# The weight of every key in columns of its own, with another order of work in the first batch: hashed attention followed by a gated feed-forward layer on one core

## The chip, the core and the metric

One NeuronCore of a Trainium2 chip runs the whole program. The metric is the time of the device in microseconds (us). The engines named below are TensorE (PE, with its weight loads listed as PEld), VectorE (DVE), ScalarE (ACT), GpSimd (POOL) and SyncE (SP), whose queue issues most of the DMAs. Each engine works through its own list of instructions in order and waits for the others by semaphores.

## The reference

```python
# q, k, v: 4 batches x 8 heads x 768 tokens x 64; proj: 64 x 6
q_bits = (einsum('bhsd,dk->bhsk', q, proj) > 0)      # 6 sign bits for each token
k_bits = (einsum('bhsd,dk->bhsk', k, proj) > 0)
mask   = bucket(q_bits)[..., :, None] == bucket(k_bits)[..., None, :]
scores = where(mask, q @ k.T / 8, -1e9)
attn   = softmax(scores)          # exp(s - max) / (sum + 1e-9)
x      = (attn @ v) as 3072 tokens x 512
g, val = x @ w_gate, x @ w_val                        # 512 -> 1536 each
ffn    = (gelu(g) * val) @ w_out                      # 1536 -> 512
out    = x + sigmoid(x @ w_res) * ffn
```

A query attends only to the keys of its own bucket. Where a query's bucket holds no key, every score is -1e9, and the softmax gives every key the same weight. The kernel needs a device for this case, and it is the part that the change rebuilds.

## The kernel before

The heads are worked in 16 pairs: pair `p` is two heads of batch `p // 4`. A pair of heads fills 128 partitions, 64 for each head. For each pair the work is as follows.

- `load` brings q, k and v from HBM (384 KB each, on SP's queue). `cast` (POOL, 0.82 us) makes bf16 copies of q and k.
- `transpose_dma` turns the bf16 copies over by a transposing DMA on SP's queue (pairs 0 and 1 use `transpose_pe` on TensorE); the result is `aug`. `move_second` (POOL) copies the second head's half into a tile `second`.
- `blocks` (DVE) transposes the fp32 data in small blocks; `hash_half` (PE) multiplies it by `projw`, a block matrix made from `proj`, and DVE turns the signs into `hb`. `spread` (PE, then a DVE copy into `bits`) lays the bits out as seven rows for each head and side, and `mask_rows` carries these rows by four small DMAs (10.5 KB each) next to the 64 rows of `aug` and into `second`. Scores of the pair can only begin when they have landed.
- `scores` runs chunk by chunk: two to four matmuls into one of two PSUM tiles `sp`, then one exp on ACT into `e` (1.02 us for 1024 columns). The seven extra rows push the score of a pair of unequal buckets far down, so that its exp is nothing.
- `values_cast` and `values_sum` (POOL) make v in bf16 with a column of ones beside it (`va`), and the sum of v over the six key tiles (`vsum`). `values` multiplies `e` by `va` and adds up in the PSUM tile `av`: for each head six query tiles of 64 values and one row sum, 390 columns.
- Before the first chunk of a head, one matmul opens the accumulation: `eps_sb`, a 128x128 tile full of 2^-90, times `vsum`. It adds the tiny weight 2^-90 for every key to every query, and so gives the mean of v where no key matches. The same 65 columns are wanted for all six query tiles, so it streams 390 columns, six times the same.
- `finish` (DVE) takes the reciprocal of the row sums and multiplies, into `x_tok`. Then `x_transpose` turns `x_tok` over into `x_sb`: in the first batch and for the last pair of a batch on TensorE with a DVE copy, otherwise by a DMA on SP's queue.

When a batch's four pairs are done, `gate_val` runs the two wide products of the feed-forward layer (for each of the two weights 48 matmuls of 512 columns and 48 of 256) with Gelu on ACT and the product on DVE. `project` (for each of six token tiles 4 matmuls `rps` for the gate, Tanh on ACT, and 12 matmuls `fps`) is a generator: `mlp_matmuls` takes a few of its matmuls at a time into the slots of the next batch's attention.

The order on each engine is the program's order: it is written out by hand. A slot is one chunk of a pair: 12 in pair 0 (one head at a time, 768 columns), 9 in every other pair. `at(slot, f, ...)` hangs a task on a slot; the main loop at the end issues a slot's scores, its tasks, some `mlp_matmuls` by a budget (`fill`), then the values of the chunk one or two slots back (`flush`). `LEAD = 4` slots of the next batch come ahead of `gate_val`, and `HELD` is the number of `project`'s matmuls that are kept back to lie beside the `finish` of the last pair. `base(p)` is the first slot of pair `p`.

Names and lines that matter here: `scores` L403 with its matmul at L408 and exp at L412; `values` L376 with the opening matmul at L385 and the others at L390; `finish` L353 to L363 (reciprocal L360, product L361); `x_transpose` L365; `mask_rows` L312 with its DMA at L319; `load` L81, its DMA at L89; `move_second` L202 (copy L204); `transpose_dma` L198 (L199); `gate_val` L417 (matmul L427, Gelu L433, product L436); `project` L441 (L449, Tanh L452, L459, L464, and the residual add on POOL L466); the table of tasks L548 to L647; the budget L649 to L663; the main loop L665 to L694. The opening matmul is

```python
nc.tensor.matmul(o, eps_sb,
    vsum[:, hi, 0:D + 1].unsqueeze(1).to_broadcast([P, T, D + 1]),
    start=True, stop=False, skip_group_check=True)
```

## Time and profile before

| what | us |
|---|---|
| five runs | 360.55, 360.68, 361.10, 362.20, 362.96; median 361.1 |
| the profiled execution: time of the device | 363.73 |
| its span in the profile | 362.0 |
| 0 to 9.1: loads, first pair's preparation, until the first exp | 9.1 |
| 9.1 to 58.2: the first batch's attention | 49.1 |
| 58.2 to 90.4, 141.9 to 174.0, 225.8 to 257.9, 306.2 to 336.6: `gate_val` of the four batches | 32.2, 32.1, 32.1, 30.4 |
| 90.4 to 141.9, 174.0 to 225.8, 257.9 to 306.2: attention of batches 1 to 3 with `project` of the batch before | 51.5, 51.8, 48.3 |
| 336.6 to 362.0: the last `project` | 25.4 |

The span is the stretch that the profile covers; the device's time is 1.73 us longer. A profile page gives busy times for each engine, the chain of waits that ended last, and groups of equal instructions with the mean of one in nanoseconds (ns). A busy time of TensorE counts the ends of overlapping matmuls, so the distance between the starts of two matmuls says more than their durations.

### The profile page before, as it was taken

How to read it: one execution, taken by the hardware profiler on the slowest of the kernel's cores; microseconds unless marked ns; L12 is line 12 of the kernel's file. 1: busy time of each engine (PE TensorE's matmuls, PEld its weight loads, DVE VectorE, ACT ScalarE, POOL GpSimd, SP SyncE). 2: the span in 40 equal slices, each digit the busy share in tenths (PEclk: the TensorE clock that was granted, in tenths of full speed). 3: DMA queues.
4: the chain of work that ended last, by engine and by line, in shares of the span. 5: the costliest groups of instructions: out<-in, count | busy, mean ns of one | idle time of the engine just before them, and what ended most of it. 6: DMA issues, size and time to landing. Idle time of an engine off the chain costs nothing.

```text
span 362.0 us, 7500 instructions
## 1 busy us (share of the span) xinstructions
PE 344.2 (95%) x3040; PEld 202.9 (56%) x3089; DVE 145.6 (40%) x213; ACT 211.3 (58%) x239; POOL 138.1 (38%) x185
## 2 busy tenths in 40 slices
PE   7896989999999999999999999999999999999994
PEld 4554565665465566666455556665555655666442
DVE  7861644333344334434343434334442123333343
ACT  5885887234788787232877777332778885232210
POOL 5978853866447258300046547400025112000000
PEclk9998999999999999999999999999999999999999
DMA  7879849997904952830003964510002210000012
GB/s 219 260 148 218 238 150 351 328 314 197 256 32 122 217 173 87 215 117 0 2 3 83 199 214 132 120 40 3 0 2 61 83 51 31 29 2 0 31 60 86
DMA packets 52574, 44.06 MB, mean 122 GB/s; under 512 B 31640, under 2 KB 44348, under 8 KB 52540
## 3 DMA queue, kind: packets, MB, share of 16 engines
q1 hardware_dynamic: 52396, 43.56, 42.8%
q8 instruction: 24, 0.39, 0.4%
q14 instruction: 10, 0.08, 0.1%
q0 software_dynamic: 64, 0.02, 0.0%
q10 hardware_dynamic: 80, 0.00, 0.0%
HBM read 29.36 MB, written 6.29 MB: 99 GB/s over the span
## 4 chain that ended last, share of the span: by engine, by line
PE 83%; DMA 5%; ACT 4%; SPq 2%; POOL 2%; issue 2%; DVE 2%; DVEq 0%; ACTq 0%; POOLq 0%
PE sp L427 34%; PE fps L459 17%; PE sp L408 13%; PE av L390 8%; PE rps L449 5%; DMA ld<-in_q_dram 3%; ACT e L412 3%; PE hs L270 3%; SPq L89 2%; PE spr L283 2%; DMA aug<-bits 1%; PE av L385 1%; ACT th L452 1%; DVE o L464 1%; DVE x_tok L361 1%
## 5 line engine op out<-in xcount | busy, mean ns | idle before, releaser
L412 ACT ACTIVATE e<-sp 128x1024 bf16<-128x1024 f32 (+1 forms) x147 | 145.0, 1007 | 40.4 <-PE sp L408 32.8
L433 ACT ACTIVATE gt<-sp 128x768 bf16<-128x768 f32 x48 | 38.9, 810 | 83.2 <-PE sp L427 83.2
L436 DVE SCALAR_TENSOR_TENSOR hh<-gt,sp 128x768 bf16<-128x768 bf16 x48 | 45.8, 954 | 81.7 <-PE sp L427 81.7
L459 PE MATMUL fps<-wo,hh 128*128 128x512 bf16 x276 | 72.7, 378 | 0.7
L390 PEld LDWEIGHTS <-e 128*128 128x128 bf16 x1152 | 52.3, 98 | 32.6 <-issue 11.2
L427 PE MATMUL sp<-x_sb,wg 128*128 128x512 bf16 (+1 forms) x377 | 70.0, 325 | 0.5
L427 PE MATMUL sp<-x_sb,wv 128*128 128x512 bf16 (+1 forms) x375 | 69.8, 324 | 0.5
L466 POOL TENSOR_TENSOR o<-o,x_tok 128x512 f32<-128x512 f32 x18 | 20.8, 1154 | 122.1 <-issue 69.4
L408 PE MATMUL sp<-aug,aug 71*128 71x512 bf16 x192 | 55.1, 330 | 5.6 <-DMA aug<-bits 3.0
L390 PE MATMUL av<-va,e 128*128 128x65 bf16 x1152 | 59.0, 194 | 1.2 <-ACT e L412 0.5
L427 PEld LDWEIGHTS <-wg 128*128 128x128 bf16 x384 | 37.4, 98 | 24.9 <-issue 0.3
L427 PEld LDWEIGHTS <-wv 128*128 128x128 bf16 x384 | 37.3, 98 | 24.5
L408 PE MATMUL sp<-second,second 128*128 128x256 bf16 (+1 forms) x174 | 47.9, 323 | 0.2
L459 PEld LDWEIGHTS <-hh 128*128 128x128 bf16 x288 | 27.6, 97 | 27.7
L464 DVE SCALAR_TENSOR_TENSOR o<-th,fps 128x512 f32<-128x512 f32 x24 | 16.4, 685 | 56.2 <-PE fps L459 54.6
L204 POOL COPY second<-aug 64x768 bf16<-64x768 bf16 x30 | 24.3, 826 | 18.0 <-DMA aug<-nat 16.1
L233 DVE STREAM_TRANSPOSE t<-ld 128x768 f32<-128x768 f32 (+1 forms) x34 | 30.0, 910 | 1.2 <-DMA ld<-in_q_dram 1.1
L449 PE MATMUL rps<-wr,x_sb 128*128 128x512 bf16 x93 | 24.5, 379 | 0.2
L452 ACT ACTIVATE th<-rps 128x512 f32<-128x512 f32 x24 | 14.3, 595 | 16.3 <-PE rps L449 13.0
L408 PEld LDWEIGHTS <-aug 71*128 71x128 bf16 x192 | 16.1, 98 | 9.0 <-DMA aug<-bits 3.2
L408 PEld LDWEIGHTS <-second 128*128 128x128 bf16 x192 | 18.7, 98 | 4.3 <-issue 1.4
L290 DVE CAST bits<-spr 128x512 bf16<-128x512 f32 (+1 forms) x24 | 15.5, 653 | 11.5 <-PE spr L283 11.3
(59 smaller groups left out, 226.1 us busy)
## 6 DMA issues: line engine op xcount, KB each, us to landing
ldv<-in_v_dram SPq DMA_DIRECT2D x16, 384.0 KB
out_dram<-o SPq DMA_DIRECT2D x24, 256.0 KB
ld<-in_q_dram SPq DMA_DIRECT2D x15, 384.0 KB
ld<-in_k_dram SPq DMA_DIRECT2D x15, 384.0 KB
ws<-in_moe_w_gate_dram SPq DMA_DIRECT2D x6, 512.0 KB
ws<-in_moe_w_val_dram SPq DMA_DIRECT2D x6, 512.0 KB
ws<-in_moe_w_out_dram SPq DMA_DIRECT2D x6, 512.0 KB
ws<-in_moe_w_res_dram SPq DMA_DIRECT2D x2, 512.0 KB
```

What stands on the lines that cost most here:

```text
L204: eng.tensor_copy(second[x[0] % NM][x[1]][D:P], aug[x][D:P])
L233: nc.vector.transpose(t32[x][:, c0:c1].rearrange("p c h n -> p (c h n)"), raw[x][:, c0:c1].rearrange("p c d -> p (c d)"))
L390: nc.tensor.matmul(o[:, qt0 + i, :], e[:, off + i * P:off + (i + 1) * P], va[:, hi, jt, 0:D + 1], start=False, stop=(jt == T - 1), skip_gr ...
L408: nc.tensor.matmul(sp[:, off:off + nq * P], ks[0:n, jt, :], qs[0:n, qt0:qt0 + nq, :], start=True, stop=True)
L412: nc.scalar.activation(e[:, 0:n], sp[:, 0:n], AF.Exp, scale=float(ALPHA))
L427: nc.tensor.matmul(sp[:, c0:c1], w[:, kk, bass.ts(m, P)], xs[:, kk, c0:c1], start=(kk == 0), stop=(kk == KM - 1))
L433: nc.scalar.activation(gt, sp[:, 0:S], AF.Gelu)
L436: nc.vector.scalar_tensor_tensor(hh[:, m, :], gt, 0.5, ps[1][:, 0:S], op0=ALU.mult, op1=ALU.mult)
L449: nc.tensor.matmul(rps, x_sb[b][:, kk, t, :], wr[:, kk, :], start=(kk == 0), stop=(kk == KM - 1))
L459: nc.tensor.matmul(fps, hh[:, m, bass.ts(t, P)], wo[:, m, :], start=(m == 0), stop=(m == KF - 1))
L464: nc.vector.scalar_tensor_tensor(o, th, 1.0, fps, op0=ALU.add, op1=ALU.mult)
L466: last.tensor_add(o3, o3, x_tok[b][:, :, t, :])
```

## The change

Four things are changed together.

1. From the second batch on, the opening matmul of a head no longer streams 390 columns into the accumulators. It writes 65 columns of its own behind them in the same PSUM bank. At the end of the pair DVE copies these 65 columns of both heads to SBUF (`share`), adds them to all six query tiles (`total`, in SBUF), and takes the reciprocal. The product into `x_tok` goes to POOL for the first three pairs of a batch and stays on DVE for the last. The first batch keeps the old form (`whole(p)`).
2. `x_transpose` of those pairs comes later: in slot 6 of the next pair instead of 4, or slot 3 instead of 2 at a batch's end. In `gate_val` the last values of the lead slots are issued ahead of the fourth k-slice of the first product instead of behind it, and 15 matmuls instead of 12 are held back for the last batch.
3. The start: `projw` is made by one POOL product from a broadcast load of `proj` and a striped tile; the first head of pair 0 is transposed alone, ahead of the hash, and ACT copies both results; the second head's cast of q goes from ACT to POOL. There are 6 warming matmuls instead of 15.
4. The table of the first batch: pair 1's steps and pair 2's casts come one slot later, some loads earlier or later (the loads of v of pair 2 and of q and k of pair 4 in slot 7 instead of 9; those of pair 5 behind the mask rows of pair 2 instead of ahead of them), `move_second` of pair 3 four slots later, the values of pair 2 earlier and of pair 3 later. `values_sum` works in place and drops an unused branch.

```diff
+    o2_pool = ctx.enter_context(tc.tile_pool(name="sums", bufs=1))
-    proj_sb = const.tile([D, NBITS], FP32, name="proj_sb")
-    nc.scalar.dma_start(proj_sb, proj)
+    proj4 = const.tile([P, 2, NBITS], FP32, name="proj4")
+    for dh, eng in ((0, nc.scalar), (1, nc.gpsimd)):
+        eng.dma_start(proj4[:, dh], proj[32 * dh:32 * dh + 32].unsqueeze(0)
+                      .to_broadcast([4, 32, NBITS]))
...
+    def whole(p):
+        return p < HP
...
-        o = av.pop(p)[:, :, 0:T * (D + 1)].rearrange("p h (t d) -> p h t d", t=T)
+        acc = av.pop(p)
+        n = T * (D + 1)
+        o = acc[:, :, 0:n].rearrange("p h (t d) -> p h t d", t=T)
+        eng = nc.vector
+        if not whole(p):
+            share = sm_pool.tile([P, 2, D + 1], FP32, tag="share", name="share")
+            nc.vector.tensor_copy(share, acc[:, :, n:n + D + 1])
+            total = o2_pool.tile([P, 2, T, D + 1], FP32, tag="total", name="total")
+            nc.vector.tensor_add(total, o,
+                                 share.unsqueeze(2).to_broadcast([P, 2, T, D + 1]))
+            o = total
+            if hp < HP - 1:
+                eng = nc.gpsimd
         rec = sm_pool.tile([P, 2, T], FP32, tag="rec", name="rec")
         nc.vector.reciprocal(rec, o[:, :, :, D])
-        nc.vector.tensor_mul(x_tok[b][:, hp].rearrange("p t (h d) -> p h t d", h=2),
-                             o[:, :, :, 0:D],
-                             rec.unsqueeze(3).to_broadcast([P, 2, T, D]))
+        eng.tensor_mul(x_tok[b][:, hp].rearrange("p t (h d) -> p h t d", h=2),
+                       o[:, :, :, 0:D], rec.unsqueeze(3).to_broadcast([P, 2, T, D]))
...
-                nc.tensor.matmul(
-                    o, eps_sb,
-                    vsum[:, hi, 0:D + 1].unsqueeze(1).to_broadcast([P, T, D + 1]),
-                    start=True, stop=False, skip_group_check=True)
+                if whole(p):
+                    nc.tensor.matmul(o, eps_sb, vs.unsqueeze(1).to_broadcast([P, T, D + 1]),
+                                     start=True, stop=False, skip_group_check=True)
+                else:
+                    nc.tensor.matmul(av[p][:, hi, n:n + D + 1], eps_sb, vs,
+                                     start=True, stop=True, skip_group_check=True)
...
                 for kk in range(KM):
+                    if m == 0 and w is wg and kk == KM - 1:
+                        meanwhile()
...
-    warm_up(9, 4)
...
+    warm_up(6, 4)
+    nc.gpsimd.tensor_mul(projw[:, :, 0:4 * NBITS].rearrange("p h (a n) -> p h a n", a=4),
+                         proj4.unsqueeze(2).to_broadcast([P, 2, 4, NBITS]),
+                         stripe.unsqueeze(1).unsqueeze(3).to_broadcast([P, 2, 4, NBITS]))
+    for side, eng, bank in ((0, nc.scalar, TP), (1, nc.gpsimd, AV)):
+        blocks((0, side), 0, T)
+        cast((0, side), eng, H0)
+        transpose_pe((0, side), bank, True)
+        new_aug((0, side))
+        transposed_head((0, side), 0, nc.scalar)
...
-    at(6, mask_rows, 1, (nc.sync, nc.gpsimd))
+    at(7, mask_rows, 1, (nc.sync, nc.gpsimd))
...
-        at(base(1) + side, move_second, (3, side))
+        at(base(1) + 4 + side, move_second, (3, side))
...
-    at(base(1) + 3, values_prep, 2)
+    at(base(1) + 1, values_prep, 2)
...
-    at(9, load, 2, (2,))
-    at(9, load, 4, (0, 1))
-    at(base(1), load, 5, (0, 1))
+    at(7, load, 2, (2,))
+    at(7, load, 4, (0, 1))
     at(base(1) + 3, load, 3, (2,))
+    at(base(1) + 4, load, 5, (0, 1))
...
-    HELD = 12
+    HELD = [0] + [12] * (B - 2) + [15]
...
-        if c == (2 if ends else 4) and p >= 1:
+        if p >= 1 and c == ((2 if whole(p - 1) else 3) if ends else 4 if whole(p - 1) else 6):
             x_transpose(p - 1, ROW if p == HP - 1 else TP)
...
-            gate_val(b - 1)
+            gate_val(b - 1, flush)
```

## The prediction, made before the changed kernel was run

> **What bounds the kernel now.** I read the page first, then the windows by stage, then the waits of one stage after the other. The page says where the end comes from:
>
> ```profile
> PE 344.2 (95%) x3040; PEld 202.9 (56%) x3089; DVE 145.6 (40%) x213; ACT 211.3 (58%) x239; POOL 138.1 (38%) x185
> ...
> PE 83%; DMA 5%; ACT 4%; SPq 2%; POOL 2%; issue 2%; DVE 2%; DVEq 0%; ACTq 0%; POOLq 0%
> ```
>
> The first line is busy time, the second the chain of waits that ended last. TensorE carries 83% of the chain. The DMA's 5% is no average: it lies in the first 34 us. The windows show the contrast between a stretch of the first batch and a whole later batch (columns: stretch, length, then busy time of PE, PEld, DVE, ACT, POOL, granted clock, DMA share, GB/s):
>
> ```profile
> 31.10:34.50 3.40, 1.12 (x7) 0.64 (x8) 0.00 (x0) 0.00 (x1) 2.93 (x5) 0.84 1.30 146
> ...
> 90.40:141.90 51.50, 50.76 (x525) 29.43 (x532) 21.58 (x32) 40.06 (x43) 28.76 (x37) 1.00 0.60 155
> 174.00:225.80 51.80, 50.86 (x526) 29.48 (x532) 21.40 (x31) 40.14 (x44) 25.56 (x33) 1.00 0.42 110
> 257.90:306.20 48.30, 47.06 (x476) 27.49 (x481) 14.31 (x22) 37.20 (x40) 11.40 (x14) 1.00 0.15 43
> ```
>
> Batches 1 to 3 are TensorE's: ACT has 11 us to spare in each, DVE 30. There a column less on TensorE is time. The first batch is ACT's, except for one hole. ACT's timeline (start, length, what; in brackets the idle time before it):
>
> ```profile
> 29.16 1.94 ACT L412 ACTIVATE e<-sp 128x1024 bf16<-128x1024 f32 x2 [0.22 <-PE sp L408]
> 34.52 1.02 ACT L412 ACTIVATE e<-sp 128x1024 bf16<-128x1024 f32 x1 [3.41 <-PE sp L408]
> 35.81 1.02 ACT L412 ACTIVATE e<-sp 128x1024 bf16<-128x1024 f32 x1 [0.27 <-PE sp L408]
> ```
>
> TensorE in turn waited there for the mask rows of pair 2, and SP's queue shows why they were late:
>
> ```profile
> 33.38 0.61 PE L408 MATMUL sp<-aug,aug 71*128 71x512 bf16 x1 [3.05 <-DMA aug<-bits]
> ```
>
> ```profile
> 21.67 1.80 SPq L89 DMA_DIRECT2D ldv<-in_v_dram  x1
> 23.53 0.45 SPq L89 DMA_DIRECT2D ld<-in_q_dram  x1
> 24.02 0.47 SPq L89 DMA_DIRECT2D ld<-in_k_dram  x1
> 24.59 0.41 SPq L89 DMA_DIRECT2D ld<-in_q_dram  x1
> 25.10 0.42 SPq L89 DMA_DIRECT2D ld<-in_k_dram  x1
> 25.61 1.77 SPq L319 DMA_DIRECT2D second<-bits  x2
> 27.48 1.48 SPq L319 DMA_DIRECT2D aug<-bits  x2
> ```
>
> The four small transfers (42 KB) stand behind five loads of 384 KB. At the 247 GB/s of the window 21.5 to 31.1, 1.92 MB take 7.8 us from 21.7, to 29.5 at the earliest; the rows landed near 33.3. And the matmul that the change shrinks:
>
> ```profile
> 139.08 0.38 PE L408 MATMUL sp<-second,second 128*128 128x256 bf16 x2
> 139.30 0.33 PE L385 MATMUL av<-vsum,eps_sb 128*128 128x390 bf16 x1
> 139.47 0.28 PE L390 MATMUL av<-va,e 128*128 128x65 bf16 x4
> ```
>
> Its listed length is 0.33, but the next one starts 0.17 after it.
>
> **What the Trainium skill says.** "TensorE: Matmul & The Clock Gate", section "Back-to-back issue gap": a warm matmul of N columns holds the array for N/2.4 + 2.5 ns, 165 ns for 390; the trace's 0.16 to 0.17 agrees. The same page ("The HAM clock gate") says that an idle time of about 3.4 us halves the clock until some 3.4 us of work have passed. The trace agrees: after the hole the 512-column score matmul is listed with 0.61 instead of 0.38 until 36.9. "GPSIMD Engine Reference", section 3.1: GpSimd needs 2.6 cycles an element with two inputs, 2.17 ns at its 1.2 GHz; L334 against L336 gives (994 - 454)/256 = 2.11 ns. "DMA: Bandwidth & Descriptors", "Issuing engines are not separate DMA queues": all queues share the same DMA engines, so bulk delays small transfers whoever issues them. In this trace only the four rows behind bulk show it.
>
> **The change, part by part.**
>
> *Opening matmul, 24 heads of batches 1 to 3.* It falls from 165 ns to what a 65-column matmul costs: sixteen L390 take 0.49 us on the chain, 31 ns each. 24 x 0.134 = 3.2 us, all in TensorE's stages.
>
> *End of a pair on DVE.* Before: reciprocal 0.23, gap 0.03, product 0.96, then `av` is free: 1.22. New: `share` reads 130 elements from PSUM; DVE's casts of 192 and 512 elements take 358 and 687 ns, 1.03 ns an element over 0.16, so 0.29; gap 0.03; `total` is the product's kind over 780 elements, 0.97: 1.29. So `av` comes free 0.07 later. TensorE stood right behind this release at 115.65 and 293.72 and near it at 128.31; three times 0.07 is 0.2 lost. DVE then still has the reciprocal, so a `bits` copy behind it is 0.3 later; five pairs have one, and TensorE's next spread asks for that bank. At 185.4, 211.6 and 269.3 that spread waited for ACT's Tanh, not for DVE; bounds 0 and 1.5, I take 0.2. Net of the first two parts: 2.8 us.
>
> *Product on POOL, nine times.* 768 elements: 454 + 640 x 2.11 = 1.80 us from L334, 454 + 640 x 1.82 = 1.62 from L466's 1154 at 512. POOL is under 56% busy in these stages. Behind it stand residual adds, `second` copies and casts, due one to two pairs later. SP's transposing DMA waits for it, but is moved two slots (2.8 us) back and thereby behind the next pair's mask rows; behind it then stand stores, transposes and loads for pairs two ahead. Cost 0. Nearest danger: pair 14, whose `x_sb` is wanted at the last `gate_val`; from slot 6 there remain two slots and 15 held matmuls, 6 us, against 1.3 of issue and a landing of about 2. I hold it covered.
>
> *Batch ends.* DVE needs 2.45 instead of 1.22 until `x_tok`; the transposes come a slot (1.4 us) later. The DVE copy (0.56) then has six matmuls (0.96) and 16 values (0.49) beside it. At 306 the 15 held matmuls (3.2 us) cover 2.45. Cost 0, bounds -0.2 and 0.4 for each end.
>
> *Start.* The first exp (9.11) moves by -0.9 to +0.5: less DVE and ACT work, but a POOL-issued load of `proj` of 128 small rows and fewer warming matmuls. It does not count: TensorE stood from 11.3 to 12.34 for `vsum` (listed as 1.0, POOL), whose v lands at 8.37 as before, with the same POOL steps behind it. The fourth exp stays at 13.2.
>
> *First batch.* Pair 1's mask rows issue a slot (about 1 us) later and on POOL behind both casts of pair 3. They were issued at 17.3 to 19.0, landing 1.7 to 1.9 later; now about 21.2, with pair 1's scores asked for at 20.8. Cost 0 to 0.8, I take 0.4. Pair 2's rows: `bits` is ready at 24.9; ahead of them now stand three loads, issued near 20, and two transposes; pair 5's loads come after. Four issues take 3.35, landing 1.8: 30.1, shifted to 30.5 by pair 1. TensorE asks at about 30.3 plus the same shift. So 3.41 shrinks to 0 to 0.8, I take 0.4; and without the hole the clock does not fall: two exps at 1.27 instead of 1.02 gain 0.5. Sum: 3.4 - 0.4 - 0.4 + 0.5 = 3.1 us. ACT then runs at its rate until 58. Next in line are the rows of pair 3, due 9 us after pair 2's start and issued 6 us ahead of need.
>
> Together 2.8 + 3.1 = 5.9. The profiled execution (span 362.0, time 363.7) would give 356.1 and 357.8. Its time stands 0.7% above the median of the runs; against that median 361.1 I forecast 355.2.
>
> **Rivals.**
>
> *Only the later batches gain.* In the first 34 us the DMA engines are 73% to 108% busy; if two transposes and three loads still hold pair 2's rows, the hole stays: 361.1 - 2.8 = 358.3. For it: transposing DMAs move little (148 GB/s in the third slice). Against: of the five loads two now come after the rows, and three are issued some 3 us earlier.
>
> *Only the first batch gains.* If DVE's and POOL's added steps at a pair's end eat the 2.8: 358.0. For it: three of eleven releases are already tight. Against: eight have 0.3 to 1.3 us of slack.
>
> *Slower: SP's queue held by a late product on POOL.* The transpose of `x_tok` waits at the head of SP's queue, and every load and mask row behind it waits too. If POOL, held by a `second` copy that itself waits for a DMA (13 such waits, 16.1 us in all), finishes more than a pair (12 us) late, the next pair's rows miss their scores. One such hole for each of three batches, priced as the one seen, (3.4 + 0.5) x 3 = 11.7: 361.1 - 5.9 + 11.7 = 366.9. It decides from 6 us of such holes on. Against it: the rows are now ahead of that transpose.
>
> *Both parts mostly void:* the hole moves to pair 1, and the tight releases eat the rest: about 361.
>
> **How the numbers follow.** Both gain 0.62 (own range 353 to 357.2), later batches only 0.14, first batch only 0.09, slower 0.10, void 0.05. Range 352.3 to 360: the low end adds the uncharged gains of the start and of the batch ends, the high end takes both half cases. Half a per cent (1.8 us) is about what a measurement tells from no change: below 359.3 lies 0.83, within 0.08, above 0.09.
>
> **What would show it.** Right: L385 with 65 columns and 0.03 to the next start; batches 1 to 3 each about 0.9 shorter; no idle of ACT above 1 us between 21 and 58, granted clock 1.00 there, and the first `gate_val` near 55. Wrong: a wait of PE's scores for `bits` rows above 1 us, TensorE waiting for DVE ahead of L385 in most pairs, SP waiting for POOL's product with loads behind it, or `gate_val` waiting for `x_sb`.

## The result, and the profile after

| | before | changed | ratio, 95% interval |
|---|---|---|---|
| median | 362.20 us (72 runs) | 359.38 us (37 runs) | 0.9929 [0.9915, 0.9943] |
| span of the profiled execution | 362.0 us | 358.3 us | |

The changed kernel is faster by 0.71%, 2.6 us of 362.2 (the quotient of the two medians, 0.9922, lies in the same interval). The forecast was 5.9 us: the direction is right, the size under half. The two profiled executions, cut at the first matmul of each stage (us):

| stage | before | changed | difference |
|---|---|---|---|
| up to the first `gate_val` | 58.02 | 56.27 | -1.75 |
| `gate_val` of batch 0 | 31.81 | 31.81 | 0 |
| attention of batch 1, then `gate_val` | 51.93, 31.69 | 51.04, 32.26 | -0.89, +0.57 |
| attention of batch 2, then `gate_val` | 52.23, 31.69 | 51.27, 31.69 | -0.96, 0 |
| attention of batch 3, then `gate_val` | 47.67, 31.46 | 47.26, 31.20 | -0.41, -0.26 |
| the last `project` | 25.46 | 25.48 | +0.02 |

So 1.94 us come from the stages that were to give 2.8, and 1.75 from the first batch, which was to give 3.1. That second number is worth little: the kernel before, run once more, reached its first `gate_val` at 55.70 instead of 58.02, without a change in it. The runs below settle the sign.

Windows of the changed kernel (stretch, length, then busy time of PE, PEld, DVE, ACT, POOL, granted clock, DMA share, GB/s), for the stretches shown of before and one more near the start:

```profile
9.00:15.00 6.00, 6.00 (x48) 3.33 (x46) 5.50 (x10) 4.21 (x8) 4.92 (x7) 0.50 0.93 326
31.10:34.50 3.40, 3.18 (x52) 2.48 (x51) 1.47 (x4) 3.25 (x4) 0.62 (x1) 1.00 0.85 265
88.65:139.25 50.60, 49.71 (x525) 28.89 (x532) 22.70 (x35) 40.08 (x44) 33.02 (x39) 1.00 0.64 159
171.95:222.80 50.85, 49.91 (x526) 28.97 (x532) 22.79 (x35) 40.34 (x44) 30.64 (x36) 1.00 0.45 112
254.90:301.75 46.85, 45.07 (x470) 26.60 (x476) 15.66 (x26) 37.10 (x40) 16.31 (x17) 1.00 0.16 44
```

In the later batches the work that left TensorE is on DVE (22.70 from 21.58) and POOL (33.02 from 28.76), which have room for it. In the stretch from 31.1 ACT works 3.25 of 3.40 us where it stood still before. But from 9 to 15 us TensorE ran at half its clock; the kernel before had 1.00 there:

```profile
9.00:15.00 6.00, 4.75 (x76) 2.88 (x69) 4.96 (x10) 4.87 (x8) 5.54 (x9) 1.00 0.93 330
```

ACT's timeline in the changed kernel (start, length, what, and in brackets the idle time before it):

```profile
10.16 1.51 ACT L433 ACTIVATE e<-sp 128x768 bf16<-128x768 f32 x2 [0.41 <-PE sp L429]
...
14.69 0.81 ACT L433 ACTIVATE e<-sp 128x768 bf16<-128x768 f32 x1
...
23.62 3.77 ACT L433 ACTIVATE e<-sp 128x1024 bf16<-128x1024 f32 x4 [0.38 <-PE sp L429]
...
31.25 5.61 ACT L433 ACTIVATE e<-sp 128x1024 bf16<-128x1024 f32 x6 [0.22 <-PE sp L429]
```

The hole ahead of pair 2 is gone: the last line runs from pair 1's end into pair 2, whose first exp is the third of its six, without a wait. But pair 1 begins at 23.62 (the third line), and the fourth exp of pair 0 is at 14.69. The kernel before had these two at 21.53 and 13.22:

```profile
13.22 1.76 ACT L412 ACTIVATE e<-sp 128x768 bf16<-128x768 f32 x2 [0.91 <-PE sp L408]
...
21.53 3.77 ACT L412 ACTIVATE e<-sp 128x1024 bf16<-128x1024 f32 x4 [0.38 <-PE sp L408]
```

A further 0.5 us goes at 43 us, where TensorE waits for constants that GpSimd makes late, and GpSimd's own timeline says why:

```profile
43.32 0.40 PE L290 MATMUL spr<-hb,sel 128*128 128x128 bf16 x4 [0.48 <-POOL sel L135]
```

```profile
35.39 0.83 POOL L197 TENSOR_SCALAR nat<-ld 128x768 bf16<-128x768 f32 x1 [3.66 <-DMA ld<-in_q_dram]
...
41.85 0.52 POOL L128 MEMSET sel<- 128x512 bf16 x1
```

GpSimd stands 3.66 us for pair 5's q, which is now loaded later. Pair 5's casts were moved by two slots with the load (the list of the change does not name them), but not far enough, and `make_sel(1)` (L128 to L135), which needs no load at all, is behind it in the queue.

The end of batch 1 shows the new opening matmul and the new tail of `finish`:

```profile
136.85 1.46 DVE L378 TENSOR_TENSOR x_tok<-total,rec 128x768 bf16<-128x768 f32 x1
136.94 0.19 PE L408 MATMUL av<-vsum,eps_sb 128*128 128x65 bf16 x1
136.97 0.28 PE L411 MATMUL av<-va,e 128*128 128x65 bf16 x4
...
137.46 1.54 POOL L199 CAST nat<-ld 128x768 bf16<-128x768 f32 x1
...
141.16 0.48 PE L451 MATMUL sp<-x_sb,wg 128*128 128x512 bf16 x2 [0.41 <-DVE x_sb L388]
```

The opening matmul has 65 columns, and the next one starts 0.03 after it, as forecast. But the product `x_tok` takes 1.46 us, beside a GpSimd cast that takes 1.54 where others take 0.82; and then `gate_val` waits 0.41 for `x_sb`. The kernel before had 0.96 for the same product, which then read `av`:

```profile
137.81 0.96 DVE L361 TENSOR_TENSOR x_tok<-av,rec 128x768 bf16<-128x768 f32 x1
```

In batch 3 a new wait stands ahead of pair 14:

```profile
274.07 0.39 PE L429 MATMUL sp<-aug,aug 71*128 71x512 bf16 x1 [0.87 <-DMA aug<-bits]
```

### The profile page after: what moved, and what is told of

Read it like the earlier page. It is cut to its first block, busy times and chain, and to the rows that moved or that the text cites. A ratio compares the mean times of both kernels' runs of the same rounds, so it can differ in the third digit from the quotient of the medians.

```text
span 358.3 us, 7540 instructions
## 1 busy us (share of the span) xinstructions
PE 341.8 (95%) x3042; PEld 202.2 (56%) x3092; DVE 152.2 (42%) x232; ACT 210.4 (59%) x234; POOL 154.1 (43%) x193
## 4 chain that ended last, share of the span: by engine, by line
PE 76%; POOL 10%; DMA 5%; DVE 3%; issue 2%; ACT 1%; SPq 1%; POOLq 0%; DVEq 0%; ACTq 0%
PE sp L451 34%; PE fps L481 14%; PE sp L429 11%; PE av L411 7%; PE rps L471 5%; PE hs L277 3%; DMA ld<-in_k_dram 2%; POOL second L211 2%; POOL ldv L335 2%; DMA aug<-bits 1%; POOL va L329 1%; PE spr L290 1%; DMA ws<-in_moe_w_gate_dram 1%; POOL nat L199 1%; POOL o L488 1%
## 5 line engine op out<-in xcount | busy, mean ns | idle before, releaser
L451 PE MATMUL sp<-x_sb,wv 128*128 128x256 bf16 (+1 forms) x376 | 69.8, 325 | 0.4
L411 PEld LDWEIGHTS <-e 128*128 128x128 bf16 x1152 | 50.4, 97 | 28.5 <-issue 9.2
L411 PE MATMUL av<-va,e 128*128 128x65 bf16 x1152 | 57.0, 193 | 0.4
L378 POOL TENSOR_TENSOR x_tok<-total,rec 128x768 bf16<-128x768 f32 x9 | 13.2, 1471 | 85.0 <-DVE rec L377 85.0
L429 PE MATMUL sp<-second,second 128*128 128x256 bf16 (+1 forms) x173 | 47.0, 319 | 0.0
L211 POOL COPY second<-aug 64x768 bf16<-64x768 bf16 x30 | 24.3, 825 | 13.2 <-DMA aug<-nat 10.3
L474 ACT ACTIVATE th<-rps 128x512 f32<-128x512 f32 x24 | 14.3, 595 | 16.1 <-PE rps L471 13.2
```

The lines of the kernel that those rows point to most:

```text
L211: eng.tensor_copy(second[x[0] % NM][x[1]][D:P], aug[x][D:P])
L411: nc.tensor.matmul(o[:, qt0 + i, :], e[:, off + i * P:off + (i + 1) * P], va[:, hi, jt, 0:D + 1], start=False, stop=(jt == T - 1), skip_gr ...
L429: nc.tensor.matmul(sp[:, off:off + nq * P], ks[0:n, jt, :], qs[0:n, qt0:qt0 + nq, :], start=True, stop=True)
L451: nc.tensor.matmul(sp[:, c0:c1], w[:, kk, bass.ts(m, P)], xs[:, kk, c0:c1], start=(kk == 0), stop=(kk == KM - 1))
```

## The experiments

The ratios are to the kernel before, timed on the same chip, each with its 95% interval. "First exp of pair 1" and the like are from the one profiled execution of each kernel.

### Which part gives, which takes

The kernel before, once more:

> The kernel before, unchanged, once more, for a second profile of it. Theory 'the first profile is typical': the hole of ACT ahead of pair 2's first exp is about 3.4 us again and the span near 362.0. Rival 'the hole varies from execution to execution and the first profile had a large one' (the profiled execution took 363.7, the median is 362.2): a hole of 1.5 to 2.5 us, a span near 360.5.

Time 361.42, span 359.6. The wait of pair 2's scores for their rows is 1.75 where the first profile had 3.05:

```profile
31.35 0.39 PE L408 MATMUL sp<-aug,aug 71*128 71x512 bf16 x1 [1.75 <-DMA aug<-bits]
```

ACT's idle time there is 1.69 instead of 3.41, and the first `gate_val` starts 2.32 us earlier. The hole that I priced was one execution's; three further kernels with the old order of the first batch had 1.14, 0.91 and 1.99.

Only the later part: the new opening matmul, `finish`, the later transposes, `gate_val` and `HELD`, with the old beginning and the old table (the lines are against the changed kernel). `values_sum` in place stays in it, in the first batch too.

```diff
-    warm_up(6, 4)
+    warm_up(9, 4)
...
-    at(7, mask_rows, 1, (nc.sync, nc.gpsimd))
+    at(6, mask_rows, 1, (nc.sync, nc.gpsimd))
...
-    at(base(1) + 4, load, 5, (0, 1))
+    at(base(1), load, 5, (0, 1))
```

> The first batch and its preparation as before, the columns of their own, the product on GpSimd and the later transposes from the second batch on as in the change. The two profiles, taken stage by stage, give this part 1.95 us: ratio 0.9946. The prediction's price was 2.8: 0.992. A rival, by which the end of a pair eats the gain: 0.998 or more.

Ratio 0.9914 [0.9881, 0.9948]. The same kernel was run once more beside the last groups:

> The old beginning and order with the new later part, once more, timed beside the other three: 0.990 to 0.993, as the first time. With the old order pair 2's hole is there (1 to 2 us) and pair 4's is small (under 0.5 us).

Ratio 0.9881 [0.9847, 0.9915]: 3.1 and 4.3 us of 361.6 and 362.4, where 2.8 was forecast. From the first `gate_val` to the end the two traces take 301.98 and 300.96 us, the two of before 303.94 each: 2.0 to 3.0 us. Whether the rest of the measured gain lies ahead of the first `gate_val` or is scatter, no run here shows.

Only the first batch: the new beginning and table, the old opening matmul and `finish` everywhere.

```diff
-                if whole(p):
-                    nc.tensor.matmul(o, eps_sb, vs.unsqueeze(1).to_broadcast([P, T, D + 1]),
-                                     start=True, stop=False, skip_group_check=True)
...
+                nc.tensor.matmul(
+                    o, eps_sb,
+                    vsum[:, hi, 0:D + 1].unsqueeze(1).to_broadcast([P, T, D + 1]),
+                    start=True, stop=False, skip_group_check=True)
```

> The new preparation and the new order of the first batch, with the old weight of every key in all batches. The two profiles give it 1.75 us: ratio 0.995. If the measured total (2.6 us) is right and the later batches give 1.95, only 0.65 are left: 0.998. The prediction's price was 3.1: 0.991.

Ratio 1.0029 [1.0008, 1.0050]: a loss of about 1 us. Pair 2's hole is gone, pair 1 begins at 23.40, and TensorE waits 1.53 for the constants:

```profile
44.16 0.40 PE L289 MATMUL spr<-hb,sel 128*128 128x128 bf16 x4 [1.53 <-POOL sel L134]
```

The parts add up: 0.990 (the mean of the two runs of the later part) times 1.0029 is 0.993, and the whole change gave 0.9929. The rival "only the later batches gain" comes nearest.

The old beginning with the new table and the new later part:

```diff
-    warm_up(6, 4)
+    warm_up(9, 4)
...
+    warm_up(6)
+    blocks((0, 1), T, HT)
```

> The change with the old preparation of pair 0 (15 warming matmuls, the half-wise copies, projw by eight small copies), but with the new order of the first batch's tasks and loads and all of the later part. Theory 'the clock': in the changed kernel TensorE's clock is granted at 0.5 from 8.3 to 15 us because it idles from 4.7 to 6.4 behind only 6 warming matmuls, and pair 1 starts at 23.6 instead of 21.5; here the clock stays at 1.00 up to 20, pair 1's first exp is near 22, and the time falls by 1.3 to 2 us against the changed kernel: ratio to before 0.988. Rival 'the order': pair 1's rows are issued a slot later and that costs the 2.1 us whatever the clock; pair 1's first exp stays at 23.3 or later and the ratio stays at 0.993.

Ratio 0.9992 [0.9963, 1.0022]. This was meant as a test of the slow clock, and the clock is not what it showed: the first 23 us ran at 1.00, and pair 1 came still later, at 25.04, since its rows, issued a slot later and with bulk loads around them, were not there:

```profile
23.91 0.61 PE L423 MATMUL sp<-aug,aug 71*128 71x512 bf16 x1 [2.84 <-DMA aug<-bits]
```

The late rows cost nothing in the changed kernel because its late start lies over them. The table is made for a later start.

### What the new beginning costs

The changed kernel with TensorE kept busy by more warming matmuls:

```diff
-    warm_up(6, 4)
+    warm_up(9, 4)
...
         cast((0, side), eng, H0)
+        if side:
+            warm_up(4, 4)
         transpose_pe((0, side), bank, True)
```

> The changed kernel whole, with 3 more warm-up groups of 4 matmuls ahead of the first batch's work and 4 more between q's and k's first-head transposes, so that TensorE is not idle from 4.7 to 6.4 us. Theory clock (the slow start is what eats the first batch's gain): the granted clock from 9 to 15 us is 1.00 instead of 0.50, pair 1's first exp is at about 21.6 us instead of 23.6, the first gate_val starts near 54.3 instead of 56.3, ratio to before about 0.987. Theory order (pair 1's mask rows are a slot later, and a slow clock only hides it): the clock is 1.00 and a wait for the mask rows of pair 1 of 1.5 to 3 us appears ahead of pair 1's first exp, which stays at 23 to 25 us; ratio 0.991 to 0.999.

Ratio 0.9940 [0.9920, 0.9961]. The clock was 1.00 up to 12 us and then fell anyway (0.58 from 12 to 16), and pair 1 began at 23.88. No long wait for pair 1's rows appeared. Both theories miss: the matmuls put in move the fall of the clock, and taking it away early does not bring pair 1 forward.

The new beginning in front of the old order of pairs 0 to 3, where only pair 5's load is moved (the edit shown further down), and the new later part:

> The new beginning in the place of the old one, with the old order of pairs 0 to 3 except for pair 5's load, and the new later part. Theory that the new beginning costs time by itself: the granted clock falls to 0.5 for 3.4 or 6.7 us before 16 us, as in the four executions with it so far, and pair 1's first exp is at 22.5 to 24 us although its mask rows come early; ratio 0.992 to 0.996. Rival (only the later order of pair 1 costs): pair 1's first exp at 21 to 22 us whatever the clock does; ratio 0.987 to 0.992.

Ratio 0.9995 [0.9974, 1.0015], against 0.9920 [0.9884, 0.9956] for the same kernel with the old beginning. Its first exps and pair 1's:

```profile
11.58 1.51 ACT L433 ACTIVATE e<-sp 128x768 bf16<-128x768 f32 x2 [1.46 <-PE sp L429]
14.89 0.81 ACT L433 ACTIVATE e<-sp 128x768 bf16<-128x768 f32 x1 [0.82 <-PE sp L429]
...
23.25 3.77 ACT L433 ACTIVATE e<-sp 128x1024 bf16<-128x1024 f32 x4 [0.38 <-PE sp L429]
```

The fourth exp is at 14.89 (13.22 before) and pair 1's first at 23.25 with its rows early. The new beginning is late by itself, but that is the smaller part of what this kernel loses in its trace: its first `gate_val` starts at 59.37, that of the kernel with the old beginning at 55.08, and of these 4.3 us 1.1 lie ahead of pair 1. The rest came with a wait of 2.27 us ahead of pair 4 (1.20 in the other) and a clock of 0.50 for 6.8 us from 52.6 on. That the slow clock is not the whole of the late start is shown by two executions further down, in which it did not fall at all in the first 23 us: pair 1 began at 23.81 and 23.19. In the seven executions with the new beginning the first exp comes at 9.3 to 11.3 and the fourth at 13.9 to 15.0 (with the old one at 8.9 to 9.6 and 12.1 to 13.8). In six of the seven k's first-head transposes wait 1.1 to 1.9 us for GpSimd's cast; that this wait is what the first exp is late by was not tried.

### GpSimd's wait for a late load

The changed kernel with `make_sel(1)` ahead of pair 5's casts:

```diff
-    at(base(2), make_sel, 1)
+    at(base(1) + 5, make_sel, 1)
```

> The changed kernel whole, with the second set of selection constants made two slots ahead of pair 5's casts on GpSimd's queue, instead of behind them. Theory head of line (GpSimd stands 3.7 us for pair 5's late load with the constants behind it): TensorE's wait for sel at 43 us (0.5 us in the changed kernel, 1.5 to 1.9 in the two others with this order) is gone, the first gate_val starts 0.3 to 1.0 us earlier, ratio 0.990 to 0.9925. Rival (another thing is late there anyway, the bits or the hash of pair 4): a wait of the same length at the same place by another name; ratio 0.993.

Ratio 0.9913 [0.9882, 0.9945], against 0.9929 [0.9915, 0.9943] for the changed kernel; the intervals overlap. TensorE's wait for `sel` is gone, and the first `gate_val` starts at 54.80 instead of 56.27. Pair 1 was 0.9 earlier in this execution (22.73), so 0.5 of the 1.5 us is this edit's.

### The batch ends

Only the later part, with the casts of pairs 10 and 14, their transposes and their copies into `second` four slots later, away from DVE's product:

```diff
-            at(s0 + i, cast, x)
+            late = 4 if p in (10, 14) else 0
+            at(s0 + late + i, cast, x)
...
-            at(s0 + 4 + i // 2, transpose_dma, x)
-            at(s0 + 8 + i, move_second, x)
+            at(s0 + late + 4 + i // 2, transpose_dma, x)
+            at(s0 + late + 8 + i, move_second, x)
```

> The old beginning with the new later part, and pair 10's and 14's casts on GpSimd four slots later, so that they run in gate_val and not beside VectorE's product of the last pair of the batch. Theory contention (VectorE and GpSimd slow each other when both read SBUF): the three products by VectorE take 0.96 us each (1.46 and 1.58 where the cast ran beside them), the cast 0.82 (1.55), TensorE's wait for x_sb at the head of the second gate_val (0.42) is gone; 0.4 to 1.0 us less than without the edit, ratio to before 0.989 to 0.991. Rival (the product is slow for the place of its operands, or the casts now hold up a load behind them on SP): the products stay at 1.46 to 1.58, or a wait for loads appears in batches 2 and 3; ratio 0.991 to 0.996.

Ratio 0.9980 [0.9961, 0.9999]: the cause is right and the remedy is wrong. The three products (count, and least, median and longest time in ns) are

```profile
L372 DVE TENSOR_TENSOR x_tok<-total,rec x3: 957/958/958, 136.0 to 300.6; 128x768 bf16<-128x768 f32 x3
```

where the changed kernel has

```profile
L378 DVE TENSOR_TENSOR x_tok<-total,rec x3: 957/1462/1577, 136.9 to 300.2; 128x768 bf16<-128x768 f32 x3
```

But the late copies into `second` now hold up pair 10's mask rows, which are written into the half of `aug` that the copies read. GpSimd's copies and SP's issue of the rows:

```profile
188.06 2.37 POOL L205 COPY second<-aug 64x768 bf16<-64x768 bf16 x3
```

```profile
185.87 3.73 SPq L320 DMA_DIRECT2D aug<-bits  x2
```

The second of the two rows goes out at 188.91, just behind the first copy's end at 188.88, so that the issue of the two takes 3.73 us instead of 1.74 in the next kernel. At 190.93 TensorE stands 0.99 us ahead of pair 10's scores; the trace names a Tanh, which had ended at 190.44. The same happens in batch 3, where the trace names the rows of pair 14 (1.59 us). From the end of one run of Gelus to the start of the next, batch 2 takes 54.56 instead of 53.55. With the copies left in their slots (`at(s0 + 8 + i, move_second, x)`) this should go; the next kernel has that, and pair 5's step from below:

> The old beginning, the new later part, pair 5's load behind pair 2's mask rows with the second selection constants early, and pair 10's and 14's casts four slots later, their copies into the second buffer where they were. Theory contention, with the copies as the cause of the loss when they were moved too: the three products by VectorE take 0.96 us, no wait for x_sb at the second gate_val, batch 2 as long as without the edit (53.6 us from the end of one run of Gelus to the next, not 54.6); 0.4 to 0.8 us less than with the load step alone, ratio to before 0.986 to 0.991. Rival (the casts themselves hold up SP's loads or GpSimd's residual adds): batch 2 stays at 54 us or more, ratio 0.993 to 0.998.

Ratio 0.9896 [0.9845, 0.9947]. The products take 957 to 958 ns, batch 1 takes 53.38 (53.88 without the step) and batch 2 53.40 (53.55): 0.65 us less; from the first `gate_val` to the end 0.43 are left (300.53 against 300.96). The same step, and early constants, on the changed kernel:

> The changed kernel whole with the second selection constants early and pair 10's and 14's casts four slots later, their copies into the second buffer where they were. Theory: as in the kernel with these two steps and the old beginning, VectorE's products 0.96 us and no wait for x_sb; the new beginning costs 0.5 to 1.5 us beside the old one, ratio 0.988 to 0.993. Rival (the new beginning costs nothing once the constants are early): ratio within 0.001 of the kernel with the old beginning.

Ratio 0.9941 [0.9917, 0.9965]. Batches 1 and 2 take 53.39 and 53.40, so the step works here too, but pair 1 began at 23.81 with the clock at 1.00, and a hole of 1.99 us stood ahead of pair 4. That is 0.0045 above the kernel with the old beginning; the two intervals overlap. A part of it goes with the clock: in ten of the 22 executions its mean over the execution was under 0.9925. The other twelve took 358.2 us in the mean, the four such executions of the kernel with the old beginning 357.2.

### What takes the place of pair 2's hole

The old beginning, the new later part, and of the new table one step, with the early constants of the kernel above:

```diff
-    at(base(1), load, 5, (0, 1))
+    at(base(1) + 4, load, 5, (0, 1))
...
-        at(base(1) + 4 + side, cast, (5, side))
-        at(base(2) + side, transpose_dma, (5, side))
+        at(base(1) + 6 + side, cast, (5, side))
+        at(base(2) + 2 + side, transpose_dma, (5, side))
...
-    at(base(2), make_sel, 1)
+    at(base(1) + 5, make_sel, 1)
```

> The old beginning with the new later part, and of the new order only one step: pair 5's q and k are loaded behind pair 2's mask rows on SP's queue, with their casts and transposes two slots later, and the second selection constants made ahead of these casts. Theory queue (SP stands at that load with the rows behind it): the hole ahead of pair 2's first exp (1.1 and 1.7 us in two runs with the old order) is gone and pair 1 stays at 21.5, so the first gate_val starts 0.9 to 1.5 us earlier than with the old beginning; ratio 0.987 to 0.989. Rival (GpSimd's wait for the late load returns it at pair 4, or the rows are late for their own landing): a wait of 1 us or more at 40 to 48 us, or the hole stays; ratio 0.990 to 0.993.

Ratio 0.9920 [0.9884, 0.9956]. The hole ahead of pair 2 is gone, as the theory has it (it is 0 in every kernel with this step), and there is no gain: a wait for pair 4's rows has come. The same step alone on the kernel before shows it without the rest:

> The kernel before with one step alone: pair 5's q and k loaded behind pair 2's mask rows, their casts and transposes two slots later, and the second selection constants ahead of these casts. No part of the new weights and nothing of the new beginning. Theory queue (the hole ahead of pair 2 is SP standing at that load): no hole ahead of pair 2's first exp, the first gate_val 1 to 1.7 us earlier than in the kernel before's usual execution; ratio 0.995 to 0.998. Rival (the time is lost again before the first gate_val, at pair 3's or 4's rows): ratio 0.998 to 1.001.

Ratio 1.0040 [1.0017, 1.0062]. TensorE's last scores of pair 3 and first of pair 4, in this kernel and then in the kernel before (second execution):

```profile
47.45 0.38 PE L408 MATMUL sp<-aug,aug 71*128 71x512 bf16 x1 [0.18 <-ACT e L412]
51.14 0.39 PE L408 MATMUL sp<-aug,aug 71*128 71x512 bf16 x1 [1.94 <-DMA aug<-bits]
```

```profile
49.53 0.38 PE L408 MATMUL sp<-aug,aug 71*128 71x512 bf16 x1 [0.18 <-ACT e L412]
51.36 0.38 PE L408 MATMUL sp<-aug,aug 71*128 71x512 bf16 x1
```

Pair 3 starts its last scores 2.08 us earlier, and pair 4 begins 0.22 earlier. That explains why nothing is gained, not why 0.4% is lost: this traced execution took 360.95 us, the median is 363.50. The loss goes with the clock. In 12 of the 22 executions the mean granted clock was under 0.9925, and these took 364.5 us in the mean; the other ten took 361.5. Of the 59 executions of the kernel before beside them two were under 0.9925, and the others took 361.3. There is no trace of such an execution of this kernel; in other kernels (the first two with the weight step below are among them) a fall to 0.50 comes with the wait ahead of pair 4 or follows it.

Over the kernels (us):

| kernel | pair 3's last scores | pair 4's first | waited there for rows |
|---|---|---|---|
| before, second execution | 49.53 | 51.36 | 0 |
| only the later part | 48.92 | 50.93 | 0.26 |
| changed | 50.38 | 52.32 | 0.18 |
| later part, load of pair 5 late | 48.32 | 51.27 | 1.20 |
| the same with late casts | 46.91 | 50.81 | 2.15 |
| before, load of pair 5 late | 47.45 | 51.14 | 1.94 |

No kernel begins pair 4 before 50.8: what is gained ahead of it is waited away there. The size of the wait differs between executions: the fourth and fifth row have the same first batch, and so have two kernels with the new beginning and early constants, with 0.30 and 1.80. Windows from 44 to 52 us of the kernel before (second execution), then of the kernel with the one step:

```profile
44.00:52.00 8.00, 7.14 (x101) 5.14 (x99) 2.86 (x5) 7.06 (x8) 5.67 (x6) 1.00 0.66 228
```

```profile
44.00:52.00 8.00, 5.80 (x94) 4.38 (x93) 1.25 (x2) 5.36 (x7) 5.69 (x6) 1.00 1.05 362
```

With the hole, the rows of pair 4 travel on DMA engines that are busy for 0.66 of the time; without it, among 2 MB of weights, at 1.05. To take the weights out of their way:

```diff
-        at(base(2) + 3, load_w)
+        at(base(2) + 1, load_w)
```

> The kernel with the two steps (old beginning, new later part, pair 5's load behind pair 2's rows with the constants early, late casts), and the first four weight loads of the feed-forward two slots earlier on SP's queue, ahead of pair 5's transposes instead of behind them. Theory bulk (pair 4's mask rows travel behind 2 MB of weights that are still landing once pair 2's hole no longer delays the rows): DMA is busy under 0.5 from 46 to 50 us, the hole of 1.9 us at 51.5 and the fall of the clock behind it are gone, the mean granted clock over the timed executions rises from 0.994 to 0.996 or more, ratio to before 0.983 to 0.988. Rival (the rows are late for their own issue on SP, 3.2 us for four): the hole stays at 1 us or more, ratio 0.988 to 0.992.

> The kernel before with pair 5's load behind pair 2's rows, the constants early, and the first four weight loads two slots earlier; no part of the new weights of keys and nothing of the new beginning. Without the weight step this was 1.004 of the kernel before, with a hole of 1.7 us ahead of pair 4 at 51.8 us. Theory bulk: that hole is gone, the first gate_val starts 1.5 to 2 us earlier than there, ratio 0.993 to 0.999. Rival (the hole moves on to pair 5's rows or to the weights' casts, or the clock falls elsewhere): ratio 1.000 to 1.005.

> The changed kernel with the constants early, pair 10's and 14's casts late, and the first four weight loads two slots earlier. Without the weight step it was 0.994, with a hole of 2.0 us ahead of pair 4 at 54.7 us and the clock at 0.5 for 6.7 us behind it. Theory bulk: that hole and that fall of the clock are gone; what stays of the new beginning is the clock before 16 us; ratio 0.986 to 0.991. Rival (the new beginning costs over 1 us of itself): ratio 0.991 to 0.995.

Ratios 0.9897 [0.9868, 0.9926], 1.0000 [0.9980, 1.0020] and 0.9929 [0.9907, 0.9951]: the theory's ratios came in none of the three, the rival's in all; pair 4 waited 1.84, 2.97 and 0.82 us for its rows. SP's queue in the first of them shows what the edit did:

```profile
38.37 0.98 SPq L170 DMA_DIRECT2D ws<-in_moe_w_val_dram  x2
39.47 5.98 SPq L200 DMA_TRANSPOSE aug<-nat  x2
45.50 0.58 SPq L90 DMA_DIRECT2D ldv<-in_v_dram  x1
46.17 1.54 SPq L320 DMA_DIRECT2D second<-bits  x2
```

Pair 5's two transposing DMAs, now behind the weights, hold SP for 5.98 us instead of 2.6, and pair 4's rows go out two us later, at 46.17 instead of 44.22; their wait was 1.84. Yet the rows landed sooner behind their issue: from the end of the last row's issue to pair 4's first scores it is 3.45, 3.25 and 3.12 us in the three kernels without the weight step and 1.79, 2.04 and 1.69 with it. So both act in these traces: the weights' bulk on the landing, by 1.2 to 1.7 us, and SP's order on the issue, which the step made 1.9 us later in the first two. The new beginning is again the dearer one by 0.0032 (0.9929 against 0.9897; the intervals overlap). The last two issue pair 4's preparation earlier:

```diff
-            at(base(2) + 2 + 2 * i + side, blocks, (4 + i, side))
-        at(base(2) + 7 + side, hash_half, 4, side)
-    for i, s in enumerate((0, 2, 3)):
-        at(base(3) + s, spread, 4, 4 * i, 4 * i + 4)
-    at(base(3) + 3, mask_rows, 4)
+            at(base(2) + 1 + 2 * i + side, blocks, (4 + i, side))
+        at(base(2) + 5 + side, hash_half, 4, side)
+    for i, s in enumerate((7, 8, 9)):
+        at(base(2) + s, spread, 4, 4 * i, 4 * i + 4)
+    at(base(3), mask_rows, 4)
```

> The kernel with the two steps (old beginning, new later part, pair 5's load behind pair 2's rows, late casts), and pair 4's blocks, hash, spread and mask rows one to three slots earlier, so that the rows go out about 3 us sooner. Theory wall (in every kernel so far pair 4's first scores start at 50.8 us or later, for their rows, and what is gained ahead of that is waited away there): the wait of 2.15 us for rows ahead of pair 4's first scores falls under 0.5, these start at 48.5 to 49.5, no fall of the clock behind it; ratio to before 0.982 to 0.988. Rival (the landing is set by the weights' 2 MB on the DMA, not by the issue): the rows land at 50 to 51 again though they went out at 41 to 44; ratio 0.988 to 0.992.

> The kernel before with pair 5's load behind pair 2's rows, the constants early, and pair 4's blocks, hash, spread and rows one to three slots earlier; nothing of the new weights of keys or of the new beginning. Theory wall: pair 4's first scores start at 48.5 to 49.5 us without a wait over 0.5, ratio 0.993 to 0.997 (1.004 without the earlier rows). Rival (DMA): the wait for rows of 1.5 us or more ahead of pair 4 stays, ratio 1.000 to 1.004.

Ratios 0.9881 [0.9838, 0.9924] and 0.9974 [0.9953, 0.9994]. The first has its rival's number, just outside the theory's. In neither did the rows go out sooner: the weights and v ahead of them held SP's queue to 46.12 in both (44.22 and 44.76 without the edit), and pair 4 waited 2.17 and 1.46. So the theory that an earlier issue brings earlier scores was not put to the test. The 0.9974 is the only gain over the kernel before that a first-batch edit brought, 0.9 us; its trace, of an execution of 363.22 us where the median is 361.15, does not show where the gain comes from.

The best kernels are the later part alone (0.9914 and 0.9881 in two measurements) and the later part with the steps above (0.9896, 0.9897, 0.9881). Their intervals do not tell them apart; the later part alone is the simplest. It beats the kernel before in both measurements. Their mean, 0.9898, also lies under the changed kernel's 0.9929 [0.9915, 0.9943], but by little more than the uncertainty of the two (0.003), and the first interval overlaps it: that the rest of the change costs something on top of the later part is likely, not proven, by this comparison.

## Why the prediction was wrong

*Opening matmul, later batches (-2.8): right.* 65 columns, the next start 0.03 later, `share` 0.29, `total` 0.97, batches 1 and 2 shorter by 0.89 and 0.96 until their ends. Alone it gave 3.1 and 4.3 us with intervals of about 1.2 to either side. GpSimd's product took 1.47, under the 1.62 to 1.80 of the estimate.

*Batch ends, "Cost 0, bounds -0.2 and 0.4 for each end": too low at one end.* The second `gate_val` stage is 0.57 longer. I took DVE's product for the old one; it had moved from a PSUM operand to an SBUF one and met GpSimd's cast. The "2.45" until `x_tok` is also a little short: its own terms, 1.29, a gap of 0.03 and 1.22, make 2.54, and the end without a cast beside it (batch 3) took 2.63, from 298.57 to 301.20.

*Pair 14: the wrong wait watched.* I watched its `x_sb`, which was in time. Its mask rows were late by 0.87 in this execution. SP's queue shows what went with it. The store ahead of these rows held SP for 1.26 us; in an execution without the wait (the later part, second time) it held it for 0.44:

```profile
271.76 1.26 SPq L477 DMA_DIRECT2D out_dram<-o  x1
```

```profile
270.44 0.44 SPq L471 DMA_DIRECT2D out_dram<-o  x1
```

Leaving out the kernel with the late copies, 13 executions have the new later part. In seven the store took 0.43 or 0.44 and there is no wait; in six it took 0.69 to 1.26, with waits of 0.29 to 0.87. Why it takes longer is not shown. Without the wait the attention of batch 3 takes 46.22 instead of 47.26.

*First batch (-3.1): the step that failed, in four terms.* The sum "3.4 - 0.4 - 0.4 + 0.5 = 3.1 us" was to be gained; the run of the first batch alone lost 1 us (1.0029).

- "3.4" was the hole of one execution, of an execution that stood 0.7% above the median, as the text said; 1.7 in the next one. The text saw the warning and took the hole in full all the same.
- "The fourth exp stays at 13.2": it came at 14.69, and pair 1 at 23.62 instead of 21.53. I held the opening matmul's wait for `vsum` to cover the start. But `vsum` was ready at 11.75 and its matmul ran at 13.15: the cover had become the earlier of the two.
- Moving pair 5's load, I followed SP's queue, which gains, and not GpSimd's, where the casts of that load stand ahead of `make_sel(1)`: 0.5 us here, 1.5 in the run of the first batch alone.
- "Next in line are the rows of pair 3": it was the rows of pair 4, which wait at 50.8 us or later for themselves. In the changed kernel this wait is 0.18. In the kernels with the old beginning, the old order and pair 5's load late it was 1.2 to 3.0. That the late start used up the room in the changed kernel is likely and not shown: two other kernels with the new beginning waited 1.80 and 2.27.

*The clock.* The forecast counted 0.5 us for a fall of the clock that goes with the hole. It did not count that the clock can fall elsewhere: from 8.3 to 15.1 us in the changed kernel's trace, and at or behind pair 4's wait in seven of the kernels above. Where pair 5's load alone is late, it falls more often than in the kernel before, and this is a cost that the forecast put at nothing.

*Rivals.* "Only the later batches gain" (358.3, at 0.14) is what happened, for another reason than the one given: the hole did go. The slower rival, SP held by the late product, did not appear: SP stood once for 2.0 us for that product, ahead of 280.1, and no hole followed.

*The signs.* Of the signs of being right the 65 columns, the start 0.03 later, the clock of 1.00 and no idle of ACT above 1 us from 21 to 58 (the longest is 0.94) came true, and the first `gate_val` came at 56.27 instead of 55: none of them covers the first 21 us, where most of the time was lost. Of the signs of being wrong `gate_val` waiting for `x_sb` came, once.

## What to carry to other kernels

Before a hole is priced, ask whether the next thing due there has room: a hole that goes brings each later due time nearer, and the first one without slack gives it back. When a load is moved later, follow not only the queue that issues it but every engine whose in-order queue holds an instruction that reads it, and what stands behind that. A hole seen in one execution is a sample; where the first profile stands above the median of the runs, look for that difference in the hole first. And compare the granted clock of all timed executions with and without a step: a step can lose by the clock where its own trace shows no loss.

## What the runs showed of the hardware

The product of the same form took 0.96 us alone and 1.46 or 1.58 beside a GpSimd cast, which itself took 1.54 instead of 0.82; with the casts moved all three products took 0.96. The Trainium skill ("SBUF — State Buffer", section "SBUF: two separate sides") says that VectorE with two SBUF inputs and a GpSimd operation that reads SBUF exclude each other from a shared pair of ports, for the whole instruction. These traces agree roughly: the product of 136.85 starts while a cast runs (136.68 to 137.51) and ends at 138.31, 0.80 behind that cast, and the next cast ends 0.69 behind the product. Alone they take 0.96 and 0.82, so the three ran nearly one after the other. In the first batch, where the product reads `av` in PSUM, it keeps 0.96 at 25.12 with a cast of 0.82 beside it.

The granted clock fell to 0.5 in the first 23 us for 6.8 us in two executions with the new beginning, for 3.4 in three and not at all in two; with the old beginning for 3.4 in four of thirteen. The lengths are multiples of 3.4, which agrees with the activity window of 3.4 us in the Trainium skill ("TensorE: Matmul & The Clock Gate", section "The HAM clock gate"), free-running by that page. The idle time of about 3.4 us that the prediction took from this section did not precede the falls: in the 3.4 us ahead of these nine TensorE is listed as busy for 1.4 to 2.5 us and idle for 1.66 at the longest. Ahead of pair 4 a wait of 1.84 us had a fall behind it and one of 1.94 had none. So what decides is not the length of one gap; the place of the window would be an explanation, but no run here controlled it.
